# How a slot's quarters share out the matmuls of the second part: more ahead of the products with v, fewer behind them

## The chip, the cores and the metric

The kernel runs on one core of a Trainium2 chip. The metric is the device time of one execution in microseconds. Before the change it was 1443.05 us (median of 5 runs, 1442.6 to 1446.73).

## The reference

```python
# batch 8, heads 8, sequence 576, head_dim 64; all float32; tau = 0.02
scores = q @ k.T / sqrt(64)                          # per batch and head
thresh = max(scores, axis=-1) - tau
scores = where(scores >= thresh, scores, -1e9)
attn   = exp(scores - max(scores)); attn = attn / (sum(attn) + 1e-9)
x      = (attn @ v), heads side by side              # (8, 576, 512)

xn  = (x - mean(x)) / sqrt(var(x) + 1e-6) * g_ln     # over the 512 features
out = x + relu(xn @ w_ch1) @ w_ch2                   # 512 -> 2048 -> 512
```

## The kernel before

The work is cut into 72 **slots**: nine for each of the 8 batches (`SLOTS = 9`), one for each pair of heads and half of the queries, and a ninth (`s == HP`) for the 64 queries per head that the halves leave over. A slot's scores fill two PSUM tiles of three banks each (`sc0`, `sc1`). VectorE takes the row maxima (line 398), ScalarE the exponentials (409), VectorE the threshold and the row sums (416), GpSimd the division (429). From the second batch on, VectorE turns the weights in 32x32 blocks (488, 494), a DMA stores them to a DRAM scratch (`scr<-et`, 500) and another fetches them in the order that the products with v need (`em<-scr`, 509, with `rest<-scr`, 510). The first batch turns them with TensorE (`tp`, `tr`).

The **products with v** of slot n run one slot later, in slot n+1 (`values_of`, line 538). They write the free end of `sc0`; ScalarE copies them to `x` (line 555, and 546 for the ninth kind), GpSimd adds them to the row sums (564).

The **second part** (layer norm and the two layers with w_ch1 and w_ch2) works on 16 groups of 288 tokens. `ffn_steps(g)` is a generator. Each of its steps is one accumulating product of 128x128 weights with 288 columns (the helper `product`, line 100, which issues two halves; the profile shows four matmul records for one such product). First come 16 feature tiles `p1` of four products each, ended by a ReLU on ScalarE (line 649), with the product for the variance (`var`) behind the ninth tile; then four output tiles `p2` of 16 products each, ended by a multiplication on VectorE (596). `p1`, `p2`, `var` and `mean` share two PSUM buffers (`ps_ff`). The generator yields 1 inside a `p1` tile and behind `var`, and 2 at the end of a `p1` tile and behind every `p2` product.

The order is written out by hand (`manual_schedule`); no scheduler moves anything. Each slot has four **quarters**, and in each the function `second_part(n, i)` issues some steps of the second part to fill TensorE between the attention's own products. How many is reckoned from `ROOM`, the weight of each quarter: what is left of the group is spread over the room that is left until the next group's x is there (`ready`). The place of the quarters in a slot, as far as TensorE's queue is concerned:

- scores of slot n (`S`), then quarter 0
- quarters 1 and 2, with the vector work of slot n between them
- products with v of slot n-1 (`V`), then quarter 3
- scores of slot n+1

On the queue of SyncE, which issues nearly all DMAs, stand in each slot: `em<-scr` and `rest<-scr` for the products with v (quarter 0), finished outputs (609), in some slots the loads of q and k (115, behind VectorE's turning of the last ones), the stores to the scratch (500), and in some slots loads of v (129, 133). `em` is one buffer, so its fetch waits for the products with v that read it last; it also waits for the stores to the scratch. The first score product of a slot waits for ScalarE's copy of the products with v (line 555), since both lie in `sc0`.

Loop at the end of a quarter's dealing (line 713 on): `got` says what the last step was, and in the first and last quarter the loop goes on until a feature tile is ended (`got` is 2).

Of the kernel before, what the change touches and what calls it, by code (L numbers as in the profile page):

```python
# [18 lines left out]
def kernel(  # L19
# [658 lines left out]

    QUARTERS = 4

    ROOM = (0.6, 1.0, 1.0, 0.6)
    STEPS = 1 + NK * ND * 2
    queue = []
    issued = 0
# [10 lines left out]
    def ready(g):  # L695

        if g < 2:
            return (24, 42)[g]
        b, t = divmod(g, 2)
        return QUARTERS * (b * SLOTS + (HP, 2 * HP)[t] + 2) + (2, 4)[t]  # L700

    def second_part(n, i):

        nonlocal issued, owed
        if not queue:
            return
        at = QUARTERS * n + i
        g = issued // STEPS
        left = sum(ROOM[t % QUARTERS] for t in range(at, ready(g + 1))) if g + 1 < NG else 0
        owed += ((g + 1) * STEPS - issued) * ROOM[i] / left if left > 0 else 8  # L710


        got = 1 if i == 0 else 2
        while queue and (owed >= 0.5 or got == 1 and i in (0, QUARTERS - 1)):
            got = next(queue[0], None)
            if got is None:
                queue.pop(0)
                got = 1
            elif got == 0:
                owed = 0.0  # L720
                break
            else:
                issued += 1
                owed -= 1
# [24 lines left out]
    for n in range(NS):  # L749
# [12 lines left out]
        conversion.fetch(2)  # L762
        run_all(stores)
        second_part(n, 0)
        next(rest, None)

# [6 lines left out]
        tick(1)  # L773
        run(n, 1)
        second_part(n, 1)
        tick(2)
        blocks_go = by_blocks(b * HP)
# [3 lines left out]
        tick(3)  # L781
        run(n, 2)
        second_part(n, 2)
        tick(4)
        box = []
# [63 lines left out]
```

## Time and profile before

| | |
|---|---|
| median of 5 runs | 1443.05 us (1444.81, 1446.73, 1442.73, 1443.05, 1442.6) |
| profiled execution: its own time, and its span | 1444.81 us, 1443.0 us |
| busy: TensorE, VectorE, GpSimd, ScalarE | 96%, 61%, 30%, 29% of the span |
| matmul records of the second part (line 100, `p`) | 8192, 1028.8 us |
| matmul records of the scores (384) and of the products with v (538) | 150.6 us and 177.3 us |
| transfer `em<-scr`, issue to landing | 5.2 / 6.0 / 7.7 us (least, median, most) |
| mean granted TensorE clock | 0.995 of full speed |

All durations come from one profiled execution; it was 1.8 us slower than the median. The 1.8 us between its time and its span lie around the first and last instruction. `L538` is line 538 of the kernel, `PE` TensorE's matmuls, `PEld` its weight loads, `DVE` VectorE, `ACT` ScalarE, `POOL` GpSimd, `SPq` SyncE's queue.

### The profile page before, as it was taken

Reading aid. Unit: us, or ns where it says so; the run is one execution under the profiler, and the core shown is the slowest. Engines: PE = TensorE matmul, PEld = TensorE weight load, DVE = VectorE, ACT = ScalarE, POOL = GpSimd, SP = SyncE. Lnnn points to the kernel's source line nnn. Section 1 sums busy time; section 2 is a strip of 40 time slices with the busy share of each in tenths; the row PEclk is TensorE's granted clock in tenths of the full one; section 3 lists DMA queues with packets and bytes.
Section 4 is the critical chain, followed back from the end, with each engine's and each line's share of the span. In section 5 each row is a group of like instructions: output and inputs, shape, how many; then the busy total and the mean of one; then the engine's idle time right before and its main releaser. Section 6 shows DMA issues by size and latency. Waiting matters only on the chain.

```text
span 1443.0 us, 29649 instructions
## 1 busy us (share of the span) xinstructions
PE 1390.2 (96%) x12168; PEld 854.9 (59%) x12168; DVE 873.8 (61%) x1492; ACT 421.7 (29%) x818; POOL 439.1 (30%) x681
## 2 busy tenths in 40 slices
PE   5879999999999999999999999999999999999998
PEld 3655665655656566655656555566556655565554
DVE  5998857556565666566665664656665566655111
ACT  3887513132222313132221312223132322213020
POOL 2444332333323233232322233232332323222100
PEclk8999999999999999999999999999999999999999
DMA  9622456557855587547855577455865578555301
GB/s 226 167 74 83 90 136 157 166 145 159 183 138 145 143 182 170 145 130 168 190 145 145 148 156 168 135 144 143 180 168 143 137 171 184 139 144 137 79 6 17
DMA packets 466840, 205.12 MB, mean 142 GB/s; under 512 B 275024, under 2 KB 428368, under 8 KB 466704
## 3 DMA queue, kind: packets, MB, share of 16 engines
q1 hardware_dynamic: 461936, 202.64, 57.7%
q8 instruction: 95, 1.56, 0.4%
q10 hardware_dynamic: 4736, 0.59, 0.4%
q14 instruction: 41, 0.34, 0.1%
q0 software_dynamic: 32, 0.00, 0.0%
HBM read 119.41 MB, written 83.76 MB: 141 GB/s over the span
## 4 chain that ended last, share of the span: by engine, by line
PE 85%; DMA 5%; DVE 5%; SPq 2%; ACT 2%; issue 1%; POOL 0%; POOLq 0%; ACTq 0%; DVEq 0%
PE p L100 64%; PE sc L538 10%; PE sc L384 9%; DMA em<-scr 2%; DVE neg L398 1%; SPq L115 1%; DVE e L416 1%; DMA v_in<-in_v_dram 1%; PE tp L100 1%; DMA et<-in_moe_w_ch_dram 1%; PE mean L100 0%; ACT e L409 0%; DVE w L263 0%; SPq L500 0%; DMA scr<-et 0%
## 5 line engine op out<-in xcount | busy, mean ns | idle before, releaser
L100 PE MATMUL p<-xc,w 128*64 128x288 f32 x4096 | 515.2, 407 | 7.4 <-ACT hidden L649 5.9
L100 PE MATMUL p<-hidden,w 128*64 128x288 f32 x4096 | 513.6, 407 | 0.0
L100 PEld LDWEIGHTS p<-xc,w 128*64 128x64 f32 x4096 | 292.2, 137 | 215.0 <-ACT hidden L649 12.6
L100 PEld LDWEIGHTS p<-hidden,w 128*64 128x64 f32 x4096 | 295.7, 137 | 198.7 <-issue 9.3
L398 DVE TENSOR_REDUCE neg<-sc 128x2 f32<-128x1152 f32 x144 | 188.8, 1352 | 249.1 <-PE sc L384 249.1
L409 ACT ACTIVATE e<-sc,neg 128x576 f32<-128x576 f32 x288 | 194.3, 741 | 296.5 <-DVE neg L398 290.1
L429 POOL TENSOR_SCALAR e<-e,den 128x576 f32<-128x576 f32 x252 | 187.9, 763 | 239.7 <-DVE den L420 239.7
L416 DVE SCALAR_TENSOR_TENSOR e<-sc,thr,e 128x576 f32<-128x576 f32 x288 | 219.1, 811 | 24.0 <-ACT e L409 24.0
L494 DVE STREAM_TRANSPOSE et<-e 128x1152 f32<-128x1152 f32 x112 | 153.6, 1375 | 77.2 <-POOL e L429 58.6
L649 ACT ACTIVATE hidden<-p 128x288 f32<-128x288 f32 x256 | 105.5, 413 | 292.3 <-PE p L100 290.9
L384 PE MATMUL sc<-kT,qT 64*128 64x384 f32 (+3 forms) x1024 | 150.6, 425 | 20.1 <-DVE qT L344 10.1
L402 POOL TENSOR_SCALAR thr<-neg,low_sb 128x2 f32<-128x2 f32 x144 | 41.6, 289 | 385.9 <-DVE neg L398 378.0
L384 PEld LDWEIGHTS sc<-kT,qT 64*128 64x128 f32 x1024 | 94.3, 191 | 77.6 <-issue 27.5
L538 PE MATMUL sc<-em,v_in 128*64 128x256 f32 (+1 forms) x1408 | 132.3, 331 | 4.5 <-DMA em<-scr 4.3
L538 PEld LDWEIGHTS sc<-em,v_in 128*64 128x64 f32 x1408 | 87.0, 138 | 44.3 <-DVE et L494 4.2
L596 DVE TENSOR_TENSOR o<-p,rb 128x288 f32<-128x288 f32 x64 | 28.4, 444 | 128.0 <-PE p L100 128.0
L555 ACT COPY x<-sc 128x256 f32<-128x256 f32 x60 | 22.3, 372 | 286.0 <-PE sc L538 280.5
L597 POOL TENSOR_TENSOR o<-o,x 128x288 f32<-128x288 f32 x64 | 51.0, 797 | 116.4 <-DVE o L596 115.0
L564 POOL TENSOR_TENSOR sum<-sum,x 128x256 f32<-128x256 f32 (+1 forms) x64 | 32.8, 513 | 95.5 <-ACT x L555 93.0
L655 POOL TENSOR_TENSOR sq<-sq 128x288 f32<-128x288 f32 x48 | 38.8, 808 | 44.0 <-ACT sq L653 41.5
L538 PE MATMUL sc<-rest,v_rest 128*64 128x256 f32 (+1 forms) x352 | 45.0, 332 | 0.0
L100 PE MATMUL tp<-diag,e 128*64 128x128 f32 x576 | 35.6, 279 | 7.1 <-ACT em L462 5.3
(130 smaller groups left out, 703.6 us busy)
## 6 DMA issues: line engine op xcount, KB each, us to landing
scr<-et SPq DMA_DIRECT2D x252, 288.0 KB, 4.6
em<-scr SPq DMA_DIRECT2D x63, 1024.0 KB, 6.0
out_dram<-ot SPq DMA_DIRECT2D x256, 36.0 KB, 4.2
q_in<-in_q_dram SPq DMA_DIRECT2D x124, 72.0 KB, 3.5
k_in<-in_k_dram SPq DMA_DIRECT2D x120, 72.0 KB, 2.6
v_in<-in_v_dram SPq DMA_DIRECT2D x64, 128.0 KB, 4.4
rest<-scr SPq DMA_DIRECT2D x63, 128.0 KB, 6.0
w<-in_moe_w_ch_dram SPq DMA_DIRECT2D x10, 512.0 KB, 6.1
```

The source lines that it names most:

```text
L100: nc.tensor.matmul(out[r], lhsT=lhsT[:, r], rhs=rhs, **flags)
L384: nc.tensor.matmul(sc[h][64 * i : 64 * i + 64 if s == HP else 128, at : at + n], lhsT=ql[r] if s == HP else qT[r, half, j * 128 : (j + 1) ...
L398: nc.vector.tensor_reduce(out=neg[:, i], in_=pairs[h], axis=AXL.X, op=ALU.max, negate=True,)
L402: nc.gpsimd.tensor_scalar(out=thr[:, i], in0=neg[:, i], scalar1=-1.0, scalar2=low_sb, op0=ALU.mult, op1=ALU.add,)
L409: nc.scalar.activation(es[:, i], blocks[i], func=AF.Exp, bias=neg[:, i : i + 1])
L416: nc.vector.scalar_tensor_tensor(out=es[:, i], in0=blocks[i], scalar=thr[:, i : i + 1], in1=es[:, i], op0=ALU.is_ge, op1=ALU.mult, accum_o ...
L429: nc.gpsimd.tensor_scalar(out=es[:, i], in0=es[:, i], scalar1=den[:, i : i + 1], scalar2=1.0, op0=ALU.mult, op1=ALU.mult,)
L494: nc.vector.transpose(et[:, :, 64 * h : 64 * h + 64].rearrange("p n (j c) -> p j n c", j=2), es[:, 2 * h : 2 * h + 2].rearrange("p j (n c) ...
L538: nc.tensor.matmul(dst[64 * h : 64 * h + 64], lhsT=vt[:, c, h, :] if c < J else vr[:, h, :], rhs=pick(em[:, c] if c < J else er, hp, h), s ...
L597: nc.gpsimd.tensor_tensor(out=o, in0=o, in1=groups[g][:, m], op=ALU.add)
L649: nc.scalar.activation(hidden[:, d], p1, func=AF.Relu)
L655: nc.gpsimd.tensor_tensor(out=sq[:, 0], in0=sq[:, 0], in1=sq[:, c], op=ALU.add)
```

## The change

Quarter 2 gets a weight of 1.25 instead of 1.0 and quarter 3 one of 0.35 instead of 0.6; the sum of a slot stays 3.2. And `got` starts at 1 in the last quarter too, so that this quarter always issues at least one step and goes on until a feature tile is ended, even when nothing is owed.

```diff
-    ROOM = (0.6, 1.0, 1.0, 0.6)
+    ROOM = (0.6, 1.0, 1.25, 0.35)
     STEPS = 1 + NK * ND * 2
...
         owed += ((g + 1) * STEPS - issued) * ROOM[i] / left if left > 0 else 8
 
 
-        got = 1 if i == 0 else 2
+        got = 1 if i in (0, QUARTERS - 1) else 2
         while queue and (owed >= 0.5 or got == 1 and i in (0, QUARTERS - 1)):
             got = next(queue[0], None)
```

## The prediction

> **What bounds the kernel now.** I read the page's first part, then TensorE's share in stretches of 100 us, then TensorE's waits, and then the order of time around the longest of them. Busy shares first, from the page and from the stretches (columns: length; busy us and records of PE, PEld, DVE, ACT, POOL; granted clock; DMA share; GB/s):
>
> ```profile
> PE 1390.2 (96%) x12168; PEld 854.9 (59%) x12168; DVE 873.8 (61%) x1492; ACT 421.7 (29%) x818; POOL 439.1 (30%) x681
> ```
> ```profile
> 500.00:600.00 100.00, 99.84 (x830) 59.80 (x828) 61.66 (x102) 24.00 (x46) 30.39 (x47) 1.00 0.69 163
> ...
> 800.00:900.00 100.00, 96.82 (x782) 58.15 (x776) 58.18 (x103) 24.37 (x48) 28.57 (x45) 0.98 0.73 162
> ...
> 1100.00:1200.00 100.00, 100.00 (x881) 60.52 (x878) 58.96 (x101) 24.25 (x47) 30.40 (x52) 1.00 0.66 156
> ```
>
> From 300 us to 1300 us TensorE has work in 99.4% of the time, so no reordering can win much there except what the stretch 800 to 900 shows: idle time, and a clock under 1.00. The change adds and removes no instruction of TensorE, so only waits, the clock and the distances between unlike products can move the time. TensorE's waits (us in total, times, longest):
>
> ```profile
> PE p L100 <- ACT hidden L649: 5.9, 5, 2.8
> ...
> PE sc L538 <- DMA em<-scr: 4.3, 4, 3.2
> ```
>
> The second line is what the change bears on: the products with v (V) wait for their weights from the scratch. The longest such wait in order of time, TensorE alone, with an undisturbed V from 170 us earlier above it:
>
> ```profile
> 709.67 11.86 PE L100 MATMUL p<-xc,w 128*64 128x288 f32 x96
> 721.36 1.90 PE L538 MATMUL sc<-em,v_in 128*64 128x256 f32 x16
> 723.09 0.60 PE L538 MATMUL sc<-rest,v_rest 128*64 128x256 f32 x4
> 723.52 0.66 PE L100 MATMUL p<-xc,w 128*64 128x288 f32 x4
> ```
> ```profile
> 876.88 11.38 PE L100 MATMUL p<-xc,w 128*64 128x288 f32 x92
> 891.43 3.21 PE L538 MATMUL sc<-em,v_in 128*64 128x256 f32 x16 [3.18 <-DMA em<-scr]
> 894.36 1.13 PE L538 MATMUL sc<-rest,v_rest 128*64 128x256 f32 x4
> 895.21 2.71 PE L100 MATMUL p<-xc,w 128*64 128x288 f32 x20
> ```
>
> Two things are seen. V waited 3.18 us. And then it ran slowly: from V's start to the next product it took 3.78 us (891.43 to 895.21) instead of 2.16 (721.36 to 723.52), and the next 20 records 2.71 us instead of 2.60; the granted clock over 891.4 to 895.2 was 0.57. That wait cost 3.18 + 1.62 + 0.11, about 4.9 us.
>
> **The measure of a step.** 96 records, 24 products, take 11.69 us from start to start (709.67 to 721.36): 0.487 us a product.
>
> **Part 1, V is moved behind more products.** 129 steps a group over 14.4 of room make 9.0 a unit of room: quarter 2 goes from 9.0 to 11.2 steps, quarter 3 from 5.4 to 3.1. In the order in which the changed kernel's instructions stand, V comes two products later than before in nearly all slots from the eleventh on (one in two of them, three in some), counted from the program's start: 0.97 us. The scores of the slots stand where they stood, within 4 products, so all of the vector work that makes the weights keeps its time, and the landing of `em` with it. Does V's own lateness delay the next `em`? Its fetch waits for V, for the stores to the scratch and for its turn on SP's queue. In the slots where V waits the fetch is issued 4.4 to 8.9 us behind the scores' start, 0.05 to 1.0 us behind the landing of the stores, while V ended some 3 us ahead of those scores. So V is not what it waits for, and landing stays.
>
> What that is worth: by the distance from one matmul's start to the next (0.24 us where V does not wait), V came late in seven slots, by 0.18, 0.59, 0.26, 0.21, 0.53, 3.35 and 0.52 us, 5.64 in all; the waits line's 4.3 counts four of them. The six short ones, 2.29 us, are under 0.97 each, and the last is the one that V gets 0.49 for; all are taken to vanish (at least 1.1, if the move brought half). The long one loses 0.97 and 2.4 are left. Whether the clock falls after 2.4 us of idleness no row tells: below 0.6 us it does not, at 3.18 it does. I take it that it does not, since 2.4 is an idle time a quarter shorter, and keep 0 and 1.73 as ends. Gain in the profiled execution: 2.29 + 0.97 + 1.73 = 5.0 us (2.1 to 5.0).
>
> The Trainium skill bears on this in "TensorE: Matmul & The Clock Gate", Part 1: the clock halves after a whole idle window of some 3.4 us, and the windows run freely. By that rule 2.4 us could never cost clock and the 1.73 go for certain; the row above, 3.18 us of reported idleness and a clock of 0.57, lies just under the rule's window, so it is no sharp bound here.
>
> **Part 2, where `p1` tiles and `var` fall.** Of the 5.9 us on ScalarE's ReLU, 2.1 are three waits of 0.70 where `var` follows the first tile of quarter 0, its ReLU held up by the exponentials:
>
> ```profile
> 731.63 0.66 PE L100 MATMUL var<-sq,avg_sb 128*64 128x288 f32 x4
> 732.99 1.19 PE L100 MATMUL p<-xc,w 128*64 128x288 f32 x8 [0.70 <-ACT hidden L649]
> ```
>
> From `var` to the next product it is 1.36 us here, 0.68 where `var` follows a later tile (564.26 to 564.94). The new order has this once instead of three times: 2 x 0.68 = 1.4 us won. Against it, in six groups V followed `var` at once (0.48 us from start to start, like `mean` and V at 1040.70 and 1041.18); now a `p1` product does, at 0.68: 6 x 0.20 = 1.2 us lost. Net 0.2 won, with ends of 1.2 lost and 1.4 won.
>
> **Part 3, what is behind V.** ScalarE's copy to `x` and the next scores, which wait for it: V at 723.09 ends at 723.69, the copy at 724.13, so 0.44 us. Behind V stand at least three products and the scores' own entry, 1.46 + 0.3 us; the cover goes from some 2.7 to 1.76 and remains. GpSimd's sums and `mean` have a whole set of scores more. Only at the end, with no scores left, it is short: `mean` of the last group starts at 1370.43, VectorE's centring runs from 1371.13 to 1372.68, and six `p2` products cover it until 1373.82; now three do, until 1372.4: 0.3 us, and a signal's way, 0.4 (0 to 0.5) lost. DMAs: in one slot of each batch one output's four stores are issued ahead of the loads of q and k instead of behind them, on SP's queue, where they fill a wait for VectorE's turning; nothing (0), and if that cover is gone, the loads come 2 us later, a slot ahead of their use. In the first batch V's copy is put behind one more ReLU on ScalarE, which is also converting weights; within 0.5 us either way.
>
> **The sum.** Profiled execution: 1444.81 - 5.0 - 0.2 + 0.4 = 1440.0 us. The median is 1.8 lower, and I lay that to smaller waits of V: its losses would be 7.4 - 1.8 = 5.6 (5.64 and 1.73 make 7.4), 2.3 short ones and 3.3 of the long sort, of which the move takes 2.7 of 5.1, 1.7 us. So 1443.05 - 2.3 - 1.7 - 0.2 + 0.4 = 1439.2 us. If all of V's losses went it would be 1437.6; if only 1.1 of the short ones and a third of the long ones went, 1441.1.
>
> A rule that speaks against reading the 96% as a bound: "Perfetto Trace Analysis", Identifying the Most-Contended Engine, says that matmul busy time is a poor measure and weight-load time a better one; here that is 59%, so by the rule there is room in TensorE's own pace. The sum above is no larger for it, since the pace of 0.487 us is the same in both kernels.
>
> **Rivals.** *The wait moves with V.* If `em` were fetched late because its buffer is free late, landing would move by the same 0.97 us and only Part 2 and the end would count: 1443.05 - 0.2 + 0.4 = 1443.3 us. For it: the fetch does wait for V in the program. Against it: the issues at 4.4 to 8.9 us above. 10%.
>
> *The scores wait for ScalarE's copy.* It decides from the point at which the copy ends over 1.76 us behind V. A ReLU (0.41) and the square of a group (1.17, line 653) both queued ahead of the copy would make it 0.44 + 0.41 + 1.17 = 2.02: 0.26 us lost in each slot where this happens, and over 64 slots up to 17 us. With 0.26 in every second slot and nothing else won but 2.3: 1443.05 + 8.3 - 2.3 = 1449.1 us. For it: the first score product waits for this copy. Against it: ScalarE is busy 29%, and a ReLU that ends before V begins has 2.16 us to pass. 10%.
>
> *The long waits stay.* If their clock loss stays as well, the short waits and 0.97 of one long one go: 1443.05 - 2.3 - 1.0 - 0.2 + 0.4 = 1440.0, and with Part 2 at its worst end, 1441.4. This is the upper part of my own case.
>
> **The numbers.** What a measurement of this kernel can tell from no change is about 0.2%, 2.9 us: below 1440.2 is faster, above 1445.9 slower. My case has 80%, of which 70 lie under 1440.2 and 10 above; with the first rival that makes same 20%, and the second slower 10%. The range that leaves out 2 in 10 is 1437.0 to 1441.7.
>
> **What would show it.** In the changed profile the waits of `sc L538` on `em<-scr` should fall from 4.3 us to under 2.5, with V some 14.8 instead of 13.8 us behind the scores in slots that load q and k; `em`'s landing should stay near 6.0 us; ReLU waits of 0.70 should be one instead of three; no wait of `sc L384` on ScalarE `x` should appear; the last group's first product should stand 2 us behind `mean` or a little more. A new line `PE sc L384 <- ACT x L555`, or an `em` wait that is as long as before, would make it wrong.

## The result and the profile after

The changed kernel takes 1441.1 us (median of 31 runs, 1438.53 to 1445.48), the kernel before over all its runs 1444.65 us (54 runs, 1440.98 to 1449.01). The ratio is 0.9976, with a 95% interval of 0.9971 to 0.9982: faster by 0.24%. Of the 3.85 us that were forecast from the first five runs, 3.5 came. The profiled execution took 1442.48 us, with a span of 1440.7; the forecast for it was 1440.0, so it kept more of its losses than the sum allowed. The page's first part, and TensorE's share in the same stretches and in one more (columns as in the prediction):

```profile
PE 1392.2 (97%) x12168; PEld 854.5 (59%) x12168; DVE 870.6 (60%) x1492; ACT 421.4 (29%) x818; POOL 438.2 (30%) x681
```
```profile
500.00:600.00 100.00, 99.24 (x828) 58.99 (x826) 60.95 (x103) 24.29 (x46) 30.41 (x48) 1.00 0.68 163
800.00:900.00 100.00, 99.95 (x820) 59.64 (x818) 63.11 (x112) 27.51 (x55) 29.00 (x47) 1.00 0.71 164
900.00:1000.00 100.00, 97.96 (x864) 59.18 (x862) 58.91 (x101) 25.08 (x50) 27.59 (x47) 0.98 0.55 145
1100.00:1200.00 100.00, 99.97 (x880) 60.49 (x878) 60.90 (x106) 25.40 (x48) 29.73 (x52) 1.00 0.64 154
```

The idle time and the lower clock that stood in 800 to 900 us are gone from there (96.82 to 99.95 busy, clock 1.00), and something like them stands in 900 to 1000. TensorE's waits in the changed kernel:

```profile
PE p L100 <- ACT hidden L649: 4.5, 3, 2.8
PE sc L538 <- DVE sq L624: 2.0, 1, 2.0
...
PE sc L538 <- DMA em<-scr: 0.4, 1, 0.4
PE p L100 <- DVE xc L579: 0.3, 1, 0.3
```

The wait on `em<-scr` fell from 4.3 us to 0.4. But the line above it, 2.0 us, is a wait of the same products, and is put down to an operation of VectorE. The order of time around it shows what it was, TensorE first and SyncE's queue below:

```profile
891.00 2.21 PE L384 MATMUL sc<-kT,qT 64*128 64x384 f32 x16
893.14 4.10 PE L100 MATMUL p<-xc,w 128*64 128x288 f32 x32
897.08 0.66 PE L100 MATMUL var<-sq,avg_sb 128*64 128x288 f32 x4
897.75 8.47 PE L100 MATMUL p<-xc,w 128*64 128x288 f32 x68
908.24 2.88 PE L538 MATMUL sc<-em,v_in 128*64 128x256 f32 x16 [2.02 <-DVE sq L624]
910.84 1.13 PE L538 MATMUL sc<-rest,v_rest 128*64 128x256 f32 x4
911.69 0.76 PE L100 MATMUL p<-xc,w 128*64 128x288 f32 x2
```
```profile
884.17 5.21 SPq L115 DMA_DIRECT2D q_in<-in_q_dram  x4
889.42 2.12 SPq L115 DMA_DIRECT2D k_in<-in_k_dram  x4
891.64 1.94 SPq L609 DMA_DIRECT2D out_dram<-ot  x4
893.67 3.89 SPq L500 DMA_DIRECT2D scr<-et  x4
902.27 0.38 SPq L509 DMA_DIRECT2D em<-scr  x1
```

The fetch of `em` was issued at 902.27, 11.3 us behind the scores, and landed at 908.14. V starts at 908.24, so it is an `em` wait like the other, whatever the line calls it. By distances from start to start, as in the prediction, V is late in four slots, by 0.23, 0.09, 2.19 and 0.54 us: 3.05 us instead of 5.64.

**Where the profiled execution's 2.3 us came from.** The spans differ by 2.3 us, of which 0.13 lie ahead of the scores at 212.5 us. Behind that, V's lateness gives 2.59; the end takes 0.46 back (from the last `p2` product to the first product of the last group 0.69 us instead of 0.24). That is 2.13 of 2.20; the new places of `var` and the slow stretches behind the long wait together moved the time by less than 0.1.

### The profile page after: what moved, and what is told of

The parts are those of the page before. It is cut to its first block, busy times and chain, and to the rows that moved or that the text cites. A ratio compares the mean times of both kernels' runs of the same rounds, so it can differ in the third digit from the quotient of the medians.

```text
span 1440.7 us, 29660 instructions
## 1 busy us (share of the span) xinstructions
PE 1392.2 (97%) x12168; PEld 854.5 (59%) x12168; DVE 870.6 (60%) x1492; ACT 421.4 (29%) x818; POOL 438.2 (30%) x681
## 4 chain that ended last, share of the span: by engine, by line
PE 90%; DVE 4%; ACT 2%; issue 1%; SPq 1%; DMA 0%; POOL 0%; POOLq 0%; DVEq 0%; ACTq 0%
PE p L100 67%; PE sc L538 10%; PE sc L384 10%; DVE e L416 1%; PE tp L100 1%; DVE neg L398 1%; ACT e L409 1%; PE mean L100 0%; PE tr L468 0%; PE var L100 0%; DMA em<-scr 0%; DVE w L263 0%; ACT em L462 0%; SPq L500 0%; DVE w L267 0%
## 5 line engine op out<-in xcount | busy, mean ns | idle before, releaser
L100 PE MATMUL p<-xc,w 128*64 128x288 f32 x4096 | 516.8, 408 | 6.5 <-ACT hidden L649 4.5
L100 PE MATMUL p<-hidden,w 128*64 128x288 f32 x4096 | 513.6, 407 | 0.0
L100 PEld LDWEIGHTS p<-xc,w 128*64 128x64 f32 x4096 | 292.0, 137 | 216.1 <-ACT hidden L649 14.5
L100 PEld LDWEIGHTS p<-hidden,w 128*64 128x64 f32 x4096 | 295.2, 137 | 199.2 <-issue 9.3
L564 POOL TENSOR_TENSOR sum<-x 128x256 f32<-128x256 f32 (+1 forms) x32 | 16.7, 521 | 97.3 <-ACT x L555 60.6
```

Source lines behind the costliest of these rows:

```text
L100: nc.tensor.matmul(out[r], lhsT=lhsT[:, r], rhs=rhs, **flags)
L564: nc.gpsimd.tensor_tensor(out=sums[g][:, cols], in0=x[:, 0, cols] if c == 1 else sums[g][:, cols], in1=x[:, c, cols], op=ALU.add,)
```

## The experiments

Each experiment ran beside the kernel before on its own chip, and every ratio is to that. The theory on trial: what the change is worth is V's wait for `em`, and nothing else. The rivals: the order of the products alone does it, or what is won is given back behind V.

**More behind V than before** (against the kernel before):

```diff
-    ROOM = (0.6, 1.0, 1.0, 0.6)
+    ROOM = (0.6, 1.0, 0.75, 0.85)
```

> The kernel before with ROOM = (0.6, 1.0, 0.75, 0.85): the products with v (V) come two products (0.97 us) earlier than before in most slots, three in some, and 7 to 11 products stand behind them instead of 5 to 9. Theory (V waits for em, and its place alone decides): in the trace of before V had under 0.97 us to spare in 23 slots; the move adds up to 0.97 in each, 18 us in all at most, less where one wait lets the transfers catch up; 0.5 to 1.2% slower than before, and the waits of V on em grow from 4.3 us to 12 to 22 us. Rival (the gain came from where p1, var and the outputs fall in the order, not from V): within 0.15% of before.

1458.58 us, 1.0109 (1.0090 to 1.0128). Its waits:

```profile
PE sc L538 <- DMA em<-scr: 14.2, 14, 1.9
```

With V two products earlier, 14 slots wait instead of four, inside the bounds of the theory (12 to 22 us). An order of products without an effect on the wait is out.

**Less behind V than after** (against the changed kernel):

```diff
-    ROOM = (0.6, 1.0, 1.25, 0.35)
+    ROOM = (0.6, 1.0, 1.5, 0.1)
```

> The kernel after with ROOM = (0.6, 1.0, 1.5, 0.1): V comes four to five products later than before, two to three later than after; behind V stands one product in 39 slots, three or four in the others. Theory: the waits of V on em that after still had (2.4 us and a slow V of 1.6) go, 1 to 3 us under after, ratio to before 0.995 to 0.9975. Rival (the scores wait for ScalarE's copy once the cover behind V is thin): the copy ends 0.44 us behind V and the cover is 0.49 + 0.3 us, so 0.35 is to spare; where a ReLU stands ahead of the copy some 0.1 to 0.3 us are lost in up to 39 slots, 4 to 12 us, ratio 0.998 to 1.006.

1444.45 us, 0.9997 (0.9988 to 1.0007): no better than the kernel before. Its waits:

```profile
PE p L100 <- ACT hidden L649: 7.3, 7, 2.8
...
PE p L100 <- DVE xc L579: 1.3, 1, 1.3
...
PE sc L538 <- DMA em<-scr: 0.4, 1, 0.4
...
PE sc L384 <- ACT x L555: 0.2, 1, 0.2
```

The theory's sum missed: of V's waits 0.4 us are left, so up to some 3.3 us are won by that, and still the time is 3.4 us over the changed kernel's. Three things took it back. In the 39 slots with one product behind V the scores come on average 0.42 instead of 0.34 us behind that product, and in each of them 0.05 us behind the end of ScalarE's copy: 39 x 0.08 = 3.1 us, too short for the waits view, which shows 0.2. Five waits of 0.68 behind `var` (against one): 4 x 0.68 = 2.7. And the end waits 1.3 us instead of 0.3. Together 6.8, where 3.3 + 3.4 = 6.7 are to be found. That is the rival's range, though ScalarE's copy to `x` is only a part of it.

**V without its wait, in both kernels.** From the second batch on V reads two tiles of weights that stand in SBUF throughout, instead of `em` and `rest`; the transfers still run, and the products take as many numbers but other ones.

```diff
         em, er = turned_weights
+        if b > 0:
+            em = w1_sb[0].rearrange("p (c a x) -> p c a x", c=J, a=4)
+            er = w1_sb[1][:, : 4 * 128].rearrange("p (a x) -> p a x", a=4)
```

> The kernel before, but from the second batch on V reads fixed tiles (converted weights of the first layer) in place of em and rest, so its products are other numbers; em and rest are fetched as ever, and every instruction stands where it stood. V cannot wait for the scratch. Theory: what V lost to em goes, 5.5 to 7.4 us with the clock: ratio to before 0.995 to 0.9965. Rival (order of p1, var and outputs): these are unchanged here, so within 0.1% of before.

> The kernel after with V reading the same fixed tiles from the second batch on. Theory: with no wait left to shorten, the place of V is worth nothing: the same time as v_free_before within 0.05%, and 1.5 to 4 us under after. Rival: it stays as far under v_free_before as after is under before, 3.5 us or 0.24%.

The kernel before without the wait: 1438.13 us, 0.9958 (0.9944 to 0.9972). The changed kernel without it: 1437.81 us, 0.9955 (0.9941 to 0.9970). All of the waits of the first that name `p L100` or the products with v:

```profile
PE p L100 <- ACT hidden L652: 6.4, 6, 2.8
PE p L100 <- DVE o L599: 0.7, 1, 0.7
PE p L100 <- ACT sq L663: 0.6, 1, 0.6
```

This is the test that decides. With the wait in both, the kernels differ by 3.5 us; without it in either, by 0.3. So the gain is V's wait on `em` with the clock that it costs, and the rest of the change (`var`, the end, the stores) is worth nothing that can be told from zero. It also gives the size: the wait cost the kernel before 6.3 us (1444.43 - 1438.13 on that chip), and costs the changed one still some 3.3 (1441.1 - 1437.8; the 1441.1 was not measured on that chip).

**Nothing behind V** (against the kernel before):

```diff
-    ROOM = (0.6, 1.0, 1.0, 0.6)
+    ROOM = (0.6, 1.0, 1.6, 0.0)
...
-        while queue and (owed >= 0.5 or got == 1 and i in (0, QUARTERS - 1)):
+        while queue and (owed >= 0.5 or got == 1 and i == 0):
```

> The kernel before with ROOM = (0.6, 1.0, 1.6, 0.0) and no step forced in quarter 3: V is followed by the next scores at once, in every slot. With one product behind V the scores' entry took 0.418 us in place of 0.336 (run q3_least): 0.08 us of waiting for ScalarE's copy. Theory of the two waits (V on em ahead, the scores on the copy behind): with no product left the wait is 0.08 + 0.49 = 0.57 us in each of 61 slots, 35 us, on top of 1438 without em waits: about 1472 us, ratio 1.012 to 1.023, and a large group of waits of sc L384 on ScalarE x L555. Rival (V's lateness alone counts): no em wait, 1438 us, ratio 0.996.

1483.89 us, 1.0258 (1.0234 to 1.0281), more than either theory expected. Its waits, and one slot in order of time, TensorE and then ScalarE:

```profile
PE sc L384 <- ACT x L555: 30.1, 58, 1.6
...
PE sc L384 <- ACT x L546: 3.7, 7, 0.5
```
```profile
1111.77 0.60 PE L538 MATMUL sc<-rest,v_rest 128*64 128x256 f32 x4
1112.87 1.47 PE L384 MATMUL sc<-kT,q_last 64*64 64x384 f32 x20 [0.50 <-ACT x L555]
```
```profile
1112.45 0.37 ACT L555 COPY x<-sc 128x256 f32<-128x256 f32 x1 [1.77 <-PE sc L538]
```

The scores start when the copy has ended (1112.82), in these waits, 58 and 7 of them. This is the wait of the prediction's second rival, at the place that it named. The copy is not late, as that rival had it: it ends 0.45 us behind V here. Only the cover is gone. The 58 sum to 30.1 us, 0.52 each. Of the 46 us over the level without `em` waits (1483.89 - 1437.8), these lines hold 33.8; of the other 12 a part is longer ReLU waits, and the rest was not traced.

**`var` inside a tile.** In the changed kernel `var` follows a whole tile and takes the other PSUM buffer, so the next product waits for the ReLU of the tile just ended. Here it is issued in the middle of the tenth tile:

```diff
+                if d == 9 and c == 1:
+                    var = ps_ff.tile([128, TOK], F32, tag="ff", name="var")
...
+                    yield 1
             nc.scalar.activation(hidden[:, d], p1, func=AF.Relu)
...
-            if d == 8:
-                var = ps_ff.tile([128, TOK], F32, tag="ff", name="var")
...
-                yield 1
```

> The kernel after with the product for the variance put into the middle of the tenth feature tile instead of behind the ninth. From var to the next product it is 0.68 us in after, because that product takes the PSUM buffer that ScalarE's ReLU of the ninth tile frees; 0.49 is a product's own pace, and once it is 1.36. Theory: 16 x 0.19 + 0.68 = 3.7 us under after, 1437.4 us, ratio 0.9940 to 0.9960. Rival (these 0.2 us are the matmul's own length and stay): as after, ratio 0.9976.

1438.91 us, 0.9949 (0.9931 to 0.9968). The distance from `var`'s last record to the next product is 0.24 us or less in all 16 groups, instead of 0.43 in 15 of them and 1.11 in one. V still waits for `em` in this execution (2.8 us in two slots and 1.0 in one), so `var` is a saving of its own.

**Less behind V where it is needed alone.** In the four slots of a batch that carry loads of q and k quarter 3 is cut to 0.15, and the old weights stand behind the last slot, for the end:

```diff
+    def room(t):
+        n, i = divmod(t, QUARTERS)
+        if n >= NS:
+            return (0.6, 1.0, 1.0, 0.6)[i]
+        return (ROOM if n % SLOTS > HP - 1 else (0.6, 1.0, 1.45, 0.15))[i]
...
-        left = sum(ROOM[t % QUARTERS] for t in range(at, ready(g + 1))) if g + 1 < NG else 0
-        owed += ((g + 1) * STEPS - issued) * ROOM[i] / left if left > 0 else 8
+        left = sum(room(t) for t in range(at, ready(g + 1))) if g + 1 < NG else 0
+        owed += ((g + 1) * STEPS - issued) * room(at) / left if left > 0 else 8
```

> The kernel after with ROOM's quarters 2 and 3 at 1.45 and 0.15 in the four slots of each batch with loads of q and k around them, and at 1.0 and 0.6 behind the last slot. V comes one to two products later still where em lands late, elsewhere as in after. Theory: of the 3.3 us that em still costs after (1441.1 against v_free_after's 1437.8) 2 to 3 go; about 20 slots have one product behind V and lose 0.08 each, 1.7 us, and var falls behind quarter 0's first tile more often, 2 to 5 times 0.68 us; the end wins 0.4. Sum: 1439.5 to 1443.5, no clear gain on after. Rival (em alone counts): 1438.5.

1441.39 us, 0.9967 (0.9954 to 0.9980), no clear gain on the changed kernel. Its waits:

```profile
PE p L100 <- ACT hidden L649: 8.0, 8, 2.8
...
PE sc L538 <- DMA em<-scr: 0.5, 1, 0.5
```

Of the `em` waits 0.5 us are left, and the wait at the end is gone; behind `var` there are six waits of 0.68, 4.1 us, where the changed kernel has one.

**Both together**, the edits of the last two:

> late_in_loads together with var in the middle of the tenth feature tile. Theory: the two add, and the position of var behind the exponentials costs less: 1441.1 - 2.5 (em) + 1.7 (scores' entry) - 3.5 (var) - 0.4 (end) = 1436.4 us, ratio 0.993 to 0.9955. Rival (the gains do not add because what is saved ahead of V makes V wait for em again): as var_mid_after or up to 2 us above it.

1438.09 us, 0.9940 (0.9922 to 0.9957): faster than both kernels, with an interval clear of the changed kernel's. Against `var` inside a tile alone (0.9949) the intervals overlap, so what the four slots add is not shown. Its time is within 0.3 us of the level without `em` waits, but that was measured on another chip, and `var`'s own saving is in it. What is left of its waits around `var` and V:

```profile
PE var L100 <- ACT hidden L656: 1.9, 6, 0.3
...
PE sc L538 <- DMA em<-scr: 1.0, 2, 0.7
```

**`var` one tile later still**, to be rid of those six waits:

```diff
-                if d == 9 and c == 1:
+                if d == 10 and c == 1:
...
-        return (ROOM if n % SLOTS > HP - 1 else (0.6, 1.0, 1.45, 0.15))[i]
+        return (ROOM if n % SLOTS > HP - 1 else (0.6, 1.0, 1.4, 0.2))[i]
```

> The kernel best with var in the middle of the eleventh instead of the tenth feature tile and 1.4 and 0.2 instead of 1.45 and 0.15 in the slots with loads. In best six var products waited 0.48 us each, 2.9 us, for the ReLU of quarter 0's first tile, which stands behind the exponentials; in the new order none of them follows that tile, and the scores have one product ahead of them in 6 slots in place of 15. Theory: 2.9 + 0.6 us under best, 1434.6 us, ratio 0.9905 to 0.9935. Rival (V, with half a product less of cover in the slots with loads, waits for em again): 1 to 4 us of it come back, 1436 to 1438 us, as best.

1442.91 us, 0.9972 (0.9957 to 0.9986): slower than the one it was made from, and more than theory and rival gave. The waits behind `var` went as expected, and V waits for `em` again. The profiled execution is the slowest of the twelve (1450.22 us), so its waits are more than the median's:

```profile
PE sc L538 <- DMA em<-scr: 6.5, 6, 2.7
...
PE sc L538 <- DVE rb L628: 2.2, 1, 2.2
```

In one slot of each batch from the third on the deal now leaves three or four products fewer behind V in the slot ahead, so the scores come earlier, while SyncE's queue is no earlier: where V waits longest, the fetch is issued 9.6 to 11.2 us behind the scores, and V waits up to 2.67 us.

## Why the prediction came near, point by point

**V later by two products, landing where it was, the short waits gone: mostly right.** In slots that load q and k V stands 14.8 us behind the scores instead of 13.8, as said, and `em` takes 5.2 / 6.0 / 7.4 us to land (5.2 / 6.0 / 7.7 before). Of the six short waits four are gone and two stayed, 0.23 us at 572.3 and 0.54 at 1058.5. In the first of these V stood no later behind its scores than before (14.0 us, before 14.3); in the second the fetch was issued 8.6 us behind the scores instead of 8.2. So "all vanish" was too much: the two products that V is moved by hold in nearly all slots, not in each, and neither does the place of the fetch.

**The long wait "loses 0.97 and 2.4 are left": wrong way, near size.** It is gone where it was, and a wait of 2.19 us stands one slot later. Where it was, V stands two products later, and `em` lands 14.3 instead of 16.6 us behind the scores: its fetch is issued 8.0 instead of 8.9 us behind them, and the transfer takes 6.2 instead of 7.7. The stores of outputs that stood ahead of the stores to the scratch there (at 873.14 on SyncE's queue) now stand ahead of the loads, but they do not explain it. In the other five batches with the same move the fetch comes 0.2 to 0.4 us later than before; the kernel before without its wait has the stores in the old place, and its `em` lands 13.4 us behind the scores; the kernel with `var` inside a tile has them in the new place, and its `em` lands at 16.4, with V 2.2 us late. So how late this one landing is differs from trace to trace, and why stays open. The queue behind that is as full as it was. The lines of the kernel before that answer to those of SyncE's queue above:

```profile
886.88 5.28 SPq L115 DMA_DIRECT2D q_in<-in_q_dram  x4
892.21 2.12 SPq L115 DMA_DIRECT2D k_in<-in_k_dram  x4
894.42 1.94 SPq L609 DMA_DIRECT2D out_dram<-ot  x4
896.46 3.89 SPq L500 DMA_DIRECT2D scr<-et  x4
```

From the first load to the end of the last store it is 13.5 us before and 13.4 after. Before, V's own wait and slow stretch had held the next scores back to 897.85, 23.1 us behind the last, and the jam met nobody; after, the next scores came on time, at 891.00, 18.2 us behind, and the jam met their V: 2.19 us. The kernel before without its wait shows that this needs no new order. Its scores come 18.0 us behind the last, the fetch 10.3 us behind them (6.4 in the kernel before), and `em` lands 16.1 us behind them, where V (which does not read it there) stands at 13.6. The scores and the fetch there:

```profile
891.60 2.21 PE L384 MATMUL sc<-kT,qT 64*128 64x384 f32 x16
```
```profile
901.94 0.38 SPq L509 DMA_DIRECT2D em<-scr  x1
```

So the step that failed is the assumption that each slot's landing holds by itself: a wait that is taken away lets the next slot run into the queue that the wait had let pass.

**The clock after "2.4 us of idleness": wrong.** It was taken not to fall, for 1.73 us. After 2.02 us it fell as it had after 3.18:

```profile
905.69:909.10 3.41, 1.39 (x14) 0.77 (x12) 3.24 (x7) 0.41 (x1) 0.00 (x0) 1.00 0.84 262
909.10:912.52 3.42, 3.42 (x19) 2.43 (x16) 0.08 (x1) 0.37 (x1) 0.00 (x0) 0.50 0.81 196
```

From V's start to the next product it was 3.45 us (908.24 to 911.69) instead of 2.16. This is the term that was mis-sized: 1.73 us were booked as won, and next to none were. With the 0.86 us of short waits that stayed, less the 0.2 by which the long one was shorter than booked (2.19 for 2.38), it makes 2.4 of the 2.5 us by which the profiled execution missed its 1440.0. What the median lost to `em`, the runs without the wait give: 6.3 us before, for which the prediction had 5.6, and 3.3 after, for which it had 1.6. So V's part was forecast at 4.0 us and came to 3.0, while the rest was forecast at 0.2 lost and came to 0.3 won, within the noise. That the totals, 3.85 and 3.5 us, lie so near is in part luck.

**`var` and `p1`: right.** The wait of 0.70 behind `var` is there once, where three were before; six groups pay the 0.20 instead:

```profile
562.42 0.65 PE L100 MATMUL var<-sq,avg_sb 128*64 128x288 f32 x4
563.78 3.62 PE L100 MATMUL p<-xc,w 128*64 128x288 f32 x28 [0.70 <-ACT hidden L649]
```

**The end: right, 0.46 us for 0.4.** Three `p2` products cover the centring, and the first product of the last group waits:

```profile
1369.04 0.66 PE L100 MATMUL mean<-sum,avg_sb 128*64 128x288 f32 x4
1369.53 1.62 PE L100 MATMUL p<-hidden,w 128*64 128x288 f32 x12
1371.44 1.92 PE L100 MATMUL p<-xc,w 128*64 128x288 f32 x14 [0.29 <-DVE xc L579]
```

**The rivals.** "The wait moves with V" is out: V's place alone, two products either way, took the wait from 4.3 us to 14.2 or to 2.4. "The scores wait for ScalarE's copy" did not come at three products behind V, begins at one (0.08 us a slot) and is most of the loss at none (0.52 us a slot). Its place was right, and 1.76 us of cover was enough, as reckoned; the late copy that it needed did not come: behind 200 us the copy ends at most 0.45 us behind V in the kernels before and after and in the runs with least and nothing behind V. "The long waits stay" is nearest to what came, 1440.0 to 1441.4 against 1441.1 measured, though the wait that stayed is another slot's. Of the change's two edits, the one of `got` moves nothing: written out, `ROOM` alone gives the changed kernel's order of instructions on every engine, and `got` alone that of the kernel before.

## What to carry to other kernels

A wait may be what lets a shared DMA queue catch up; before booking its removal, follow the queue one step further and ask who arrives at it earlier. Work that hides two waits on one engine (here products ahead of V and behind it) is a balance with two edges: the experiments with more, less and nothing behind V priced both, while setting it slot by slot won nothing that can be told from the changed kernel (0.9967 against 0.9976). To know what a change of order can win at all, take the wait away in both kernels and compare: it gave 0.3 us where the kernels themselves gave 3.5, and 1437.8 us as the time that is left when this wait is gone.

## What the runs showed of the hardware

**The clock is judged by fixed windows.** Between 60 us and the last slots, every fall of the granted clock in these runs is to half and lasts 3.41 us, and the falls of one run lie on one grid of that length. Reckoned by that grid, the idle time inside one window (gaps of over 0.5 us) decides, and not the length of the wait. All windows with 2.02 us or more were followed by one at half clock (2.02, 2.02, 2.22, 2.33, 2.40 and 2.87 us, in four kernels); of those between 1.89 and 1.96 some were and some were not; below that none was. A wait of 2.06 us in the kernel with `var` inside a tile, which a window's edge cut to 1.84, cost no clock:

```profile
885.67:889.08 3.41, 1.57 (x14) 0.67 (x10) 2.76 (x2) 0.41 (x1) 1.64 (x3) 1.00 0.88 213
889.08:892.49 3.41, 3.19 (x30) 2.51 (x32) 0.00 (x0) 0.37 (x1) 0.31 (x1) 1.00 0.70 114
```

The Trainium skill, "TensorE: Matmul & The Clock Gate", Part 1, has free-running windows of about this length, and these runs agree; it asks for a whole idle window, and here 2.02 of 3.41 us, 59%, were enough. So whether a wait of about 2 us costs another 1.7 us (3.41 us at half clock) is a matter of where it falls.

**Waits scatter the times.** The kernels in which V waits for `em` for long spread over 7 to 14 us from run to run (7.0 changed, 8.0 for the kernel before over all runs, 7.6 with more behind V, 8.0 with `var` inside a tile, 13.7 with `var` one tile later); those with 1.0 us of it or less stay within 1.0 to 2.0 us (both without the wait, least and nothing behind V, less behind V in four slots, and that together with `var` inside a tile). These have 4 to 11 runs each, while the kernels before and after have 54 and 31, which widens their spread; but the other three with long waits have 6 to 12. That fits the windows, but that they are the cause was not tested.
